# Wider conversions of the gated block's input weights, and Gram products of a block diagonal k, in a recurrence with two mixing blocks

## The chip, the cores and the metric

The kernel runs on one core of one Trainium2 chip, in one launch. The metric is the device time of that launch in microseconds (us), the median over several runs. The engines are named as the profile names them: PE is TensorE (PEld its weight loads), DVE is VectorE, ACT is ScalarE, POOL is GpSimd, SP is SyncE, which issues the transfers.

## The reference

Three stages follow each other, all in float32. The first is a recurrence with a state of 48x48 for each of 4 batches and 8 heads, over 768 steps:

```python
k_n = k / (np.linalg.norm(k, axis=-1, keepdims=True) + 1e-06)
for t in range(S):
    kt, vt, bt = (k_n[:, :, t], v[:, :, t], beta[:, :, t, None])
    y[:, :, t] = np.einsum('bhd,bhde->bhe', q[:, :, t], state)
    v_old = np.einsum('bhde,bhd->bhe', state, kt)
    state = state + bt[:, :, :, None] * np.einsum('bhd,bhe->bhde', kt, vt - v_old)
```

The second is a gated block: h = relu(x @ w_in) with w_in of 384 x 1024; half of h is u, the other half is normalized over its 512 columns, mixed over the 768 tokens by w_spatial, shifted by b_spatial and multiplied by u; the product goes through w_out. The third forms theta = x @ w_theta, mixes x cos(theta) and x sin(theta) over the tokens by two 768 x 768 matrices, adds x, and adds relu(u @ w_ch).

## The kernel before

**The recurrence in chunks.** The 768 steps are cut into 12 chunks of 64 for each batch, 48 chunks in all, counted g = 0 to 47; all 8 heads are worked on together, two on each half of the 128 partitions as four pairs (HP = 4). Eight chunks make a round (RM = 8), so there are six rounds. For a round, `norms` forms the norms of k, `gram` forms the products of k with k (and with q) within a chunk, and `invert` inverts all the round's unit triangular matrices at once on VectorE, row by row (L730 and L742). For a chunk, `chain` does what really depends on the chunk before: ru from the state (L842, L843), rt (L846), the solve with the inverse in GX (L853, L854), copies into W, the update of the state s (L869, L871), copies back into W, and the output py (L881, L882). Here "the solve" of a chunk is L853 and L854, and rt stands just ahead of it.

**Gram products.** In rounds 0 and 1 a Gram has 64 columns. From round 2 on (`FUSE = 2`) it is fused: k times k and k times q in one product of 128 columns, for 32 chunks. For each of the four pairs there are two matmuls, one on the upper left and one on the lower right quarter of the array (L670 to L672). A matmul on f32 operands is one instruction in the program and two in the trace; a transpose, and a matmul on the rounded type float32r, is one in both.

**The gated block and the third stage.** Each large product is made of three matmuls on float32r parts (high x high, high x low, low x high) in `mm_tasks` (L982). `load_w1` brings w_in, whose values arrive as float64 words: `f64_to_f32` makes float32 out of the two 32-bit halves by one instruction on ScalarE and four on VectorE (L903, L905, L907, L909), and `split` makes the two parts (a copy on ScalarE or VectorE, a subtraction at L916 on VectorE or GpSimd). The other weights go through the same conversion in the background (`park`, tiles bgr and bgm) and lie in DRAM until the third stage reads them.

**What sets the order.** Every operation is a task with a cost, a priority and the engines that may do it. A planner (`Plan.run`) goes through them at build time with these costs, picks engine and place for each, and emits the instructions in that order. On the chip each engine works its own list in order and waits on semaphores. The attention tasks have priorities of the chunk's number, the background conversions 500 and up, the large matmuls 1000 and up. On TensorE the planner also keeps an account of how busy the array is: where it expects the clock to fall, it puts in padding transposes of the identity (`filler`, L506), or prefers a large matmul. A task's `act` and `mode` tell it how busy a product keeps the array and how the array is divided for it.

**Buffers.** Rings of buffers are shared by name: in the kernel before, the raw words of w_in lie in the ring vh (six buffers) and the float32 values in vl (six buffers).

## Time and profile before

| | |
|---|---|
| median of 3 runs | 807.64 us (804.51 to 813.95) |
| the profiled execution | 808.91 us |
| its span, first to last instruction | 807.1 us |
| mean granted TensorE clock | 0.972 of full speed |
| busy share PE, DVE, ACT, POOL | 93%, 77%, 42%, 19% |
| chain that ended last, by engine | PE 60%, DVE 23%, DMA 6%, issue 4%, ACT 4% |

The profiled execution takes 1.8 us more than its span. The shares are means over two different halves, so the profile is read by stage: rt of chunk 0 starts at 38.6 us, that of chunk 12 (the second batch) at 164.9 us, that of chunk 47 (the last) at 440.2 us, and the first matmul that writes y starts at 493.0 us. A busy share of TensorE holds the latency of each matmul, so two starts are compared where a cost is wanted.

### The profile page before, as it was taken

The page shows a single profiled execution, that of the slowest core. Times are in us where ns is not written, and L with a number is a line of the kernel's source. Part 1 is how long each engine was busy: PE and PEld are TensorE (multiplying, and loading weights), DVE is VectorE, ACT ScalarE, POOL GpSimd, SP SyncE. Part 2 cuts the span into 40 slices and gives each one's busy share as a digit, 9 for nine tenths or more (in the row PEclk, how much of TensorE's full clock was granted, in tenths as well). Part 3 has the DMA queues.
Part 4 walks back from the last instruction along what each step waited for, and adds up shares of the span by engine and source line. Part 5 has one row for each costly group of instructions (what it writes and reads, how often), then busy time and mean ns, then how long its engine had stood idle before and what let it go on. Part 6 is the DMA issues. An engine that isn't in the chain of part 4 may idle for free.

```text
span 807.1 us, 21948 instructions
## 1 busy us (share of the span) xinstructions
PE 749.4 (93%) x8904; PEld 684.7 (85%) x8904; DVE 622.8 (77%) x1543; ACT 342.3 (42%) x763; POOL 155.9 (19%) x175
## 2 busy tenths in 40 slices
PE   5289889999999989999999999999999999999998
PEld 5277668778987867888878999999999999999997
DVE  5999998999997898998887564779566575556545
ACT  3636336536424444642755243355333342333321
POOL 2026622533112232211111000012111111111100
PEclk9799889999998998999999999999999999999999
DMA  7726624464575876578785710153010011002001
GB/s 219 219 65 191 177 83 140 130 171 130 185 217 171 236 230 193 156 217 245 211 240 174 222 57 14 66 175 119 20 67 27 28 42 58 26 24 75 1 1 59
DMA packets 84996, 102.42 MB, mean 127 GB/s; under 512 B 8992, under 2 KB 65568, under 8 KB 84896
## 3 DMA queue, kind: packets, MB, share of 16 engines
q1 hardware_dynamic: 84896, 101.03, 42.1%
q8 instruction: 70, 1.15, 0.6%
q14 instruction: 30, 0.25, 0.1%
HBM read 74.38 MB, written 22.41 MB: 120 GB/s over the span
## 4 chain that ended last, share of the span: by engine, by line
PE 60%; DVE 23%; DMA 6%; issue 4%; ACT 4%; SPq 2%; POOL 1%; POOLq 0%; DVEq 0%; ACTq 0%
PE m L982 29%; PE y L982 19%; DVE un L742 5%; DVE tmp L730 4%; PE mg L506 2%; PE gp L672 2%; DMA bgr<-in_w_r_dram 2%; ACT GX L474 2%; PE py L881 1%; PE ru L853 1%; DVE kq L800 1%; PE ru L842 1%; DVE GX L683 1%; DVE bgm L907 1%; PE s L869 1%
## 5 line engine op out<-in xcount | busy, mean ns | idle before, releaser
L982 PE MATMUL m<-w,vh 128*128 128x256 f32 x576 | 110.8, 292 | 0.2 <-ACT uT L474 0.2
L982 PEld LDWEIGHTS m<-w,vh 128*128 128x128 f32 x576 | 89.7, 192 | 3.5 <-issue 0.9
L982 PE MATMUL y<-wr,xTh 128*128 128x384 f32 x432 | 86.2, 337 | 0.0
L982 PE MATMUL y<-w,xTl 128*128 128x384 f32 x432 | 83.9, 336 | 0.0
L982 PE MATMUL m<-w,vl 128*128 128x256 f32 x288 | 81.9, 284 | 0.8 <-POOL vl L916 0.5
L982 PEld LDWEIGHTS y<-wr,xTh 128*128 128x128 f32 x432 | 75.3, 188 | 0.0
L982 PEld LDWEIGHTS y<-w,xTl 128*128 128x128 f32 x432 | 75.1, 188 | 0.0
L742 DVE TENSOR_TENSOR un<-un,tmp 128x30 f32<-128x30 f32 (+21 forms) x209 | 69.2, 342 | 1.1
L730 DVE TENSOR_TENSOR tmp<-un 128x30 f32<-128x30 f32 (+21 forms) x209 | 65.2, 322 | 1.2
L982 PEld LDWEIGHTS m<-w,vl 128*128 128x128 f32 x288 | 55.3, 192 | 1.2 <-POOL vl L916 0.7
L1301 DVE TENSOR_SCALAR bgr<-m 128x384 int32<-128x384 f32 x22 | 12.2, 555 | 55.1 <-PE m L982 55.1
L474 ACT ACTIVATE W<-ru 64x192 f32<-64x192 f32 x88 | 28.5, 324 | 44.7 <-PE ru L854 43.5
L982 PE MATMUL m<-xTh,wih 128*128 128x256 f32 x144 | 46.3, 322 | 0.0
L982 PE MATMUL m<-wo,gh 128*128 128x384 f32 x176 | 44.7, 334 | 0.0
L650 POOL TENSOR_TENSOR gm<-mask,ng 128x256 f32<-128x256 f32 x53 | 36.4, 690 | 41.5 <-DVE pp L693 18.5
L818 POOL TENSOR_TENSOR vk<-vk,ng 128x384 f32<-128x384 f32 x25 | 24.1, 964 | 96.8 <-DMA vk<-in_vkn_dram 63.3
L853 PEld LDWEIGHTS ru<-rt,GX 64*64 64x64 f32 x384 | 26.2, 136 | 18.1 <-DVE rt L846 13.7
L853 PE MATMUL ru<-rt,GX 64*64 64x48 f32 x384 | 32.2, 224 | 9.7 <-DVE rt L846 9.0
L506 PE MATMUL mg<-ident 128*128 128x128 f32 x231 | 38.2, 302 | 3.1 <-ACT GX L474 1.4
L982 PE MATMUL m<-xTl,wih 128*128 128x256 f32 x144 | 40.6, 282 | 0.0
L982 PE MATMUL m<-xTh,wil 128*128 128x256 f32 x144 | 40.6, 282 | 0.0
L672 PE MATMUL gp<-kg 48*64 48x128 f32 x512 | 37.5, 290 | 3.2 <-DVE pp L693 1.8
(207 smaller groups left out, 2063.0 us busy)
## 6 DMA issues: line engine op xcount, KB each, us to landing
kq<-in_kqT_dram SPq DMA_DIRECT2D x96, 128.0 KB, 3.7
vk<-in_vkn_dram SPq DMA_DIRECT2D x48, 192.0 KB, 3.7
kg<-in_kqT_dram SPq DMA_DIRECT2D x32, 256.0 KB, 3.3
gd<-gt SPq DMA_DIRECT2D x24, 256.0 KB, 2.5
graw<-gd SPq DMA_DIRECT2D x24, 256.0 KB, 3.0
k<-in_vkn_dram SPq DMA_DIRECT2D x24, 192.0 KB, 3.0
xd<-xs SPq DMA_DIRECT2D x48, 96.0 KB, 2.8
xr<-xd SPq DMA_DIRECT2D x24, 192.0 KB, 3.6
```

Source lines behind the costliest of these rows:

```text
L474: nc.scalar.activation(out=out, in_=in_, func=func, **kw)
L506: nc.tensor.transpose(MGt[:, 256:384], ident.t, ident.t)
L650: eng[e].tensor_tensor(out=gm.t, in0=mask.t.unsqueeze(1).to_broadcast([128, HP, CH]), in1=ng_b[r].t[:, j, 1].unsqueeze(2).to_broadcast([12 ...
L672: mm(out=pv()[o:o + 64, hp, :], lhsT=kh, rhs=kg.t[i:i + D, :, hp, :] if fused else kh, start=True, stop=True)
L683: nc.vector.scalar_tensor_tensor(out=GXt[1][:, u0 + hp], in0=GXt[1][:, u0 + hp], scalar=ng_b[1].t[:, j, 1, hp:hp + 1], in1=mask.t, op0=ALU ...
L730: eng[e].tensor_tensor(out=t3, in0=un.t[:, k:k + 1, 0:k].to_broadcast([128, m, k]), in1=un.t[:, t0:32:st, k:k + 1].to_broadcast([128, m, k ...
L742: eng[e].tensor_tensor(out=un.t[:, t0:32:st, 0:k], in0=un.t[:, t0:32:st, 0:k], in1=t3, op=ALU.add)
L800: A(o_dve(256), lambda e, p0=p0, i=i: nc.vector.tensor_tensor(out=kq.t[p0:p0 + 64, i], in0=gpv(ps)[p0:p0 + 64], in1=gm.t[p0:p0 + 64], op=A ...
L818: lambda e: eng[e].tensor_tensor(out=vk.t, in0=vk.t, in1=ng_b[r].t[:, j].unsqueeze(3).to_broadcast([128, 2, HP, D]), op=ALU.mult), [ng_b[r ...
L853: mm(out=pu.t[64:128, hp, :], lhsT=gx[64:128, u, :], rhs=rt.t[64:128, hp, :], start=True, stop=True)
L982: mm(out=view(), lhsT=a, rhs=c, start=(start and q == 0 and s_ == 0), stop=(stop and q == tot - 1 and s_ == 2))
L1301: P.add(o_dve(DM), lambda e: nc.vector.tensor_scalar(out=ni.t.bitcast(I32), in0=th(), scalar1=1.0 / TWO_PI, scalar2=None, op0=ALU.mult), [ ...
```

## The change

There are two edits, and a third that makes room for them. The fused Gram copies k of a chunk into a tile BD of 128 x 4 x 128, whose two diagonal blocks hold the two head halves and whose other blocks stay zero; then one matmul on the whole array does what two on quarters did. The two copies go to ScalarE or GpSimd, as the planner picks. The planner's cost for a fused Gram goes from 925 to 460 ns, its `act` from 0.35 to 0.93, its `mode` from 1 (quarters) to 0 (whole array). The input weights are converted 512 columns at a time, with the raw words in the ring uT (three buffers of 4 KB a partition) and the values in whole vl buffers. The tile sr is gone (the root is written into ng), and tmp is 240 columns wide.

```diff
+    BD = single("pa", "bd", [128, HP, 128])
+    BDh = [Buf(tile_=BD.t) for _ in range(2)]
...
-    r_sr = ring("pa", "sr", [128, RM, HP], F32, 1)
...
-    r_tmp = ring("pa", "tmp", [128, 256], F32, 2)
+    r_tmp = ring("pa", "tmp", [128, 240], F32, 2)
...
+    A([("POOL", 900.0)], lambda e: nc.gpsimd.memset(BD.t, 0.0), (), BDh, -25.0, port=False)
...
-        A([("ACT", 120.0)], lambda e: act(sr.t, ss.t, ACTF.Sqrt), [ss], [sr], p0 + 0.6, crit=r < 1)
+        A([("ACT", 120.0)], lambda e: act(ng.t[:, :, 1], ss.t, ACTF.Sqrt), [ss], [ng], p0 + 0.6, crit=r < 1)
...
             for hp in range(HP):
+                if fused:
+                    mm(out=pv()[:, hp, :], lhsT=BD.t[:, hp, :], rhs=kg.t[:, :, hp, :], start=True, stop=True)
+                    continue
                 for o, i in ((64, 0), (0, 64)):
-                    kh = kg.t[i:i + D, 0, hp, :] if fused else kg.t[i:i + D, hp, :]
-                    mm(out=pv()[o:o + 64, hp, :], lhsT=kh, rhs=kg.t[i:i + D, :, hp, :] if fused else kh, start=True, stop=True)
-
-        mt = A(o_pe(925 if r >= FUSE else 490), f, [kg], [ps], pr, crit=r < 1, act=0.35 if r >= FUSE else 0.292)
+                    kh = kg.t[i:i + D, hp, :]
+                    mm(out=pv()[o:o + 64, hp, :], lhsT=kh, rhs=kh, start=True, stop=True)
+
+        if fused:
+
+            for p0, c0, bd in ((0, 64, BDh[0]), (64, 0, BDh[1])):
+                A([("ACT", d_acts(256)), ("POOL", 480.0)], lambda e, p0=p0, c0=c0: copy(e, BD.t[p0:p0 + 64, :, c0:c0 + 64], kg.t[p0:p0 + 64, 0]),
+                  [kg], [bd], pr, part=p0)
+        mt = A(o_pe(460 if fused else 490), f, [kg] + (BDh if fused else []), [ps], pr, crit=r < 1, act=0.93 if fused else 0.292,
+               mode=0 if fused else 1)
...
-    r_cvr = Ring(pools, "pm", [128, 256, 2], I32, "vh", 6)
-    r_cvr.items = r_vh.items
-    r_cvm = Ring(pools, "pm", [128, 256], F32, "vl", 6)
+    r_cvm = Ring(pools, "pm", [128, DF], F32, "vl", 6)
...
+    r_cvr = Ring(pools, "pm", [128, DF, 2], I32, "uT", 3)
+    r_cvr.items = r_uT.items
...
-        for c0 in (DF, 0):
+        for c in (DF, 0):
             for kk in range(KX):
-                for c in (c0, c0 + 256):
-                    pr = (WP0 + 0.1 * n) if n < 6 else 0.5 + 0.3 * n
...
-                    m = f64_to_f32(r_cvr.new, r_cvm.new, w_in[kk * 128:(kk + 1) * 128, c:c + 256], 256, pr)
...
+                pr = (WP0 + 0.1 * n) if n < 3 else 0.5 + 0.6 * n
+                n += 1
+                m = f64_to_f32(r_cvr.new, r_cvm.new, w_in[kk * 128:(kk + 1) * 128, c:c + DF], DF, pr)
```

Since the planner orders everything anew, the lists of all engines change. On TensorE, early in the recurrence, the list before has two Grams in a row (16 matmuls in the program, gp from kg on 64 rows) between ru of a chunk (L842, L843) and the large matmuls of the gated block (m from the parts wih and wil of w_in):

```order
L843 MATMUL ru<-W_110,kq 64x48
L842 MATMUL ru<-W_110,kq 64x48
L843 MATMUL ru<-W_110,kq 64x48
L672 MATMUL gp<-kg 64x128 x16
L982 MATMUL m<-wih_139,xTh 128x512
L982 MATMUL m<-wil_142,xTh 128x512
```

In the changed list, a Gram there (four matmuls on the whole array, from kg and bd) stands between large matmuls, which are L992 now, and the output py (L892, L893):

```order
L992 MATMUL m<-wil_144,xTh 128x512
L992 MATMUL m<-wih_141,xTl 128x512
L673 MATMUL gp<-kg,bd 128x128 x4
L892 MATMUL py<-kq,W_110 48x64
L893 MATMUL py<-kq,W_110 48x64
```

Eight matmuls of a Gram have become four, and other work stands on either side of it. On VectorE, at the start of the inversion of round 2, the list before has the conversion of w_in (vl, 256 columns) between the inversion's steps (un and tmp, L730 and L742):

```order
L905 TENSOR_SCALAR vl<-vl 128x256
L730 TENSOR_TENSOR tmp<-un 128x30
L903 TENSOR_SCALAR vl<-vl 128x256
L742 TENSOR_TENSOR un<-un,tmp 128x30
L907 SCALAR_TENSOR_TENSOR vl<-vh,vl 128x256
L730 TENSOR_TENSOR tmp<-un 128x58
L909 SCALAR_TENSOR_TENSOR vl<-vh,vl 128x256
L742 TENSOR_TENSOR un<-un,tmp 128x2x29
```

In the changed list, just ahead of the same inversion (L719 is its transpose, the former L708), the same operations are L914, L916, L918 and L920 on 512 columns:

```order
L918 SCALAR_TENSOR_TENSOR vl<-uT,vl 128x512
L916 TENSOR_SCALAR vl<-vl 128x512
L920 SCALAR_TENSOR_TENSOR vl<-uT,vl 128x512
L918 SCALAR_TENSOR_TENSOR vl<-uT,vl 128x512
L480 CAST wih_140<-vl 128x512
L920 SCALAR_TENSOR_TENSOR vl<-uT,vl 128x512
L719 STREAM_TRANSPOSE un<-GX_112 128x1024
```

There are half as many of them, twice as wide, and two blocks are converted before the inversion starts. On GpSimd the copies of k stand among the masks gm (L652, the former L650) and the scalings of vk:

```order
L652 TENSOR_TENSOR gm<-mask,ng 128x256
L480 COPY bd<-kg 64x4x64
L652 TENSOR_TENSOR gm<-mask,ng 128x256 x2
L480 COPY bd<-kg 64x4x64
L829 TENSOR_TENSOR vk<-vk,ng 128x384
L652 TENSOR_TENSOR gm<-mask,ng 128x256 x2
```

No copy of k stood on this list before.

## Rows read from the trace of the kernel before

**Rows 1.** Busy time by stage: length, then us of PE, PEld, DVE, ACT, POOL

```profile
38.60:164.90 126.30, 113.17 (x1958) 94.48 (x1956) 118.55 (x353) 59.12 (x140) 55.15 (x64) 0.93 0.46 129
164.90:440.20 275.30, 259.22 (x4377) 219.15 (x4378) 248.43 (x637) 132.31 (x308) 60.22 (x66) 0.97 0.69 201
440.20:493.00 52.80, 52.80 (x412) 50.23 (x412) 32.54 (x75) 19.95 (x38) 2.21 (x4) 1.00 0.36 111
493.00:807.10 314.10, 309.82 (x1872) 307.67 (x1871) 194.15 (x360) 110.53 (x226) 33.69 (x29) 1.00 0.16 51
```

**Rows 2.** The large matmuls (L982) alone, by stage: PE, PEld, clock, DMA

```profile
164.90:440.20 275.30, 142.99 (x814) 111.16 (x815) 0.97 0.69 201
440.20:493.00 52.80, 51.76 (x380) 49.18 (x380) 1.00 0.36 111
```

**Rows 3.** Chain that ended last, from 440 us: start, us, what

```profile
444.49 48.49 PE m L982 x354
492.98 1.05 PE y L982 x6
```

**Rows 4.** Timeline, ru of one chunk: start, us, instruction

```profile
231.44 0.22 PE L842 MATMUL ru<-W,kq 48*64 48x48 f32 x1
231.45 0.22 PE L843 MATMUL ru<-W,kq 48*64 48x48 f32 x1
...
231.50 0.22 PE L842 MATMUL ru<-W,kq 48*64 48x48 f32 x1
231.51 0.22 PE L843 MATMUL ru<-W,kq 48*64 48x48 f32 x1
```

**Rows 5.** Timeline, one fused Gram and the matmul behind it

```profile
117.45 1.09 PE L672 MATMUL gp<-kg 48*64 48x128 f32 x16
118.47 0.39 PE L982 MATMUL m<-xTh,wih 128*128 128x256 f32 x1
```

**Rows 6.** Padding transposes (L506) in two stretches: PE, PEld, clock, DMA

```profile
38.70:42.10 3.40, 3.40 (x18) 3.40 (x17) 0.50 0.00 0
42.20:46.90 4.70, 4.70 (x44) 4.52 (x42) 1.00 0.01 3
```

**Rows 7.** Groups of instructions by shape, VectorE: xcount, busy us, mean ns

```profile
L907 DVE SCALAR_TENSOR_TENSOR bgm<-bgr,bgm 128x384 int32<-128x384 int32 x34 | 22.0, 648 | 0.3
...
L903 DVE TENSOR_SCALAR bgm<-bgm 128x384 f32<-128x384 f32 x34 | 14.7, 433 | 6.8 <-ACT bgm L474 6.7
...
L916 DVE TENSOR_TENSOR vl<-hv,vh 128x512 fp32r<-128x512 f32 x14 | 9.4, 688 | 1.0 <-ACT vh L474 0.9
...
L907 DVE SCALAR_TENSOR_TENSOR vl<-vh,vl 128x256 int32<-128x256 int32 x12 | 5.4, 450 | 0.0
...
L916 DVE TENSOR_TENSOR wil<-vl,wih 128x256 fp32r<-128x256 f32 x9 | 5.2, 575 | 0.0
...
L903 DVE TENSOR_SCALAR vl<-vl 128x256 f32<-128x256 f32 x12 | 4.1, 353 | 0.0
...
L905 DVE TENSOR_SCALAR vl<-vl 128x256 int32<-128x256 int32 x12 | 3.8, 316 | 0.1
```

**Rows 8.** Subtractions for the tile gl: ns min/median/max, first and last start

```profile
L916 DVE TENSOR_TENSOR gl<-graw,gh x15: 679/1585/1691, 455.9 to 753.3; 128x512 fp32r<-128x512 f32 x15
L916 POOL TENSOR_TENSOR gl<-graw,gh x9: 1287/1290/1293, 560.9 to 753.2; 128x512 fp32r<-128x512 f32 x9
```

**Rows 9.** Padding transposes (L506) by stage: PE, PEld, clock, DMA

```profile
38.60:164.90 126.30, 35.21 (x220) 26.69 (x219) 0.93 0.46 129
164.90:440.20 275.30, 2.88 (x11) 1.30 (x11) 0.97 0.69 201
```

**Rows 10.** Waits from 100 to 440 us, PE's and DVE's longest

```profile
PE ru L853 <- DVE rt L846: 7.4, 10, 1.4
...
DVE rt L846 <- PE ru L843: 7.9, 9, 2.3
```

**Rows 11.** The tile kg: what its readers' engine waited for

```profile
  DMA kg<-in_kqT_dram: 0.2, 1
```

More of the change, by code (lines that the diff above doesn't have):

```diff
@@ L608, in norms @@
         p0 = (r - 2) * RM + NPR if r > 1 else -20.0 if r == 0 else -10.0
-        ss, sr = r_ss.new(), r_sr.new()
+        ss = r_ss.new()
         ng = ng_b[r] = r_ng.new()
@@ L626, in f2 @@
             n, ga = ng.t[:, :, 0], ng.t[:, :, 1]
-            nc.vector.reciprocal(out=n, in_=sr.t)
+            nc.vector.reciprocal(out=n, in_=ga)
             nc.vector.tensor_tensor(out=n, in0=n, in1=ss.t, op=ALU.mult)
-            nc.vector.tensor_tensor(out=n, in0=n, in1=sr.t, op=ALU.add)
+            nc.vector.tensor_tensor(out=n, in0=n, in1=ga, op=ALU.add)
             nc.vector.tensor_scalar(out=n, in0=n, scalar1=0.5, scalar2=1e-6, op0=ALU.mult, op1=ALU.add)
@@ L1019, in m_V @@
               for kk in range(KX)]
-        wr = [x for kk in range(KX) for c in (2, 3) for x in wiq[kk, c]]
+        wr = [x for kk in range(KX) for x in wiq[kk, 1]]
         mm_tasks(ps, lambda: ps.t, gr, DF, [hi, lo] + wr, pr)
@@ L1073, in m_U @@
                   for kk in range(KX)]
-            wr = [x for kk in range(KX) for x in wiq[kk, f // 2]]
+            wr = [x for kk in range(KX) for x in wiq[kk, 0]]
             mm_tasks(ps, lambda ff=ff: v3()[:, ff, :], gr, TG, [hi, lo] + wr, pr, per=UPER)
```

11 lines of the change are left out of this document (5 added, 6 removed).

## The prediction

> **What bounds the kernel now.** I read the busy time by stage first. The program has two halves. Until the 48th chunk of the recurrent part is solved (440.2 us) no engine is saturated alone: between 164.9 and 440.2 us, the last 35 chunks, VectorE is busy 248.43 of 275.3 us and TensorE 259.22 [rows 1]. From there to the end TensorE alone decides: 52.8 of 52.8 us and 309.8 of 314.1 us, with VectorE at about 62% [rows 1]. The chain of waits confirms it: one piece of 48.49 us, 354 matmuls of the gated block without a break, then the second mixing block's y [rows 3]. The waits in the first half show what the two engines do there: TensorE waits for VectorE's rt (7.4 us), VectorE for TensorE's ru (7.9 us) [rows 10]. Neither queue runs ahead of the other; the recurrence passes between them, and each has other work standing in front of it.
>
> So the time is the moment of the last solve plus the TensorE work still left then. A large matmul (L982) before that moment fills a hole; one after it costs its full 51.76 / 380 = 0.136 us [rows 2].
>
> **Gram products.** Before, each fused Gram issues 16 instructions on 64x64 quarters, two at a time: in the rows of ru, which have the same form with 48 columns, two instructions on opposite quarters start 0.01 us apart and the next pair 0.06 us later [rows 4]. A Gram of 16 takes 118.47 - 117.45 = 1.02 us until the next matmul starts [rows 5], so eight pairs at some 0.11 us and the edges. After, 8 full-array instructions of 128 columns. The trace has such a thing, the padding transposes on the identity, 128x128 in f32: 44 in 4.70 us at full clock, 0.107 us each, and 18 in 3.40 us at half [rows 6]. Eight of those are 0.86 us. The two quarters already ran side by side, and a full-array instruction takes as long as a pair. The edges depend on neighbours and I count none: the new product stands among quarter-sized matmuls as often as the old one stood among large ones. Bounds: 0.46 us saved per Gram if the diff's figure (460 instead of 925) were true, 32 x 0.46 = 14.9 us; nothing saved, or some tenths lost, if weights of 128 columns are not hidden. I take zero, the transposes being the nearest row and carrying 128-column weights themselves.
>
> The Trainium skill, TensorE: Matmul & The Clock Gate, section Back-to-back issue gap, gives N/2.4 + 2.5 ns between matmuls, 56 ns for 128 columns; by it the new Gram would be 0.45 us and the sum some 14 us lower. The 0.107 us of the transposes speaks against it for f32.
>
> Against that stands new work: 64 half copies of k into the block diagonal tile, 33 on ScalarE and 31 on GpSimd in the program's order. ScalarE is busy 132.31 of 275.3 us [rows 1], which hides its share. If a ScalarE copy waits for k or for the earlier Gram, the copies of W stand behind it, and the recurrence with them; k lands early enough now (the Gram waited 0.2 us for it in all) [rows 11], so I add nothing. GpSimd is not free of cost: when it subtracts for gl, VectorE's own subtraction for gl has a median of 1585 ns where its shortest is 679 [rows 8]. Bounds for 31 copies: nothing, if they fall beside VectorE work that reads PSUM, and 31 x 0.91 = 28 us at the gl rate. I take 1 us, near the lower end: a copy is half as wide on half the partitions, and the order spreads the copies over 32 chunks.
>
> The Trainium skill, GPSIMD Engine Reference, section Specifications, says that GpSimd shares its SBUF interfaces with VectorE and collides with instructions that have two SBUF inputs; most of the inversion is of that kind. By that rule alone the upper bound is the nearer one; the gl rows agree with its direction, and no row has the price of such a copy.
>
> **Input weights.** Twelve conversions of 256 columns become six of 512. On VectorE: 12 x (353 + 316 + 2 x 450) ns = 18.8 us, taking L909 like L907, plus 9 subtractions of 575 ns = 5.2 us, in all 24.0 us [rows 7]. The wider forms by the step from 256 to 384 columns, 80 ns for L903 and 198 ns for L907 [rows 7], taken twice: 6 x (513 + 476 + 2 x 846) = 16.1 us, plus 4 subtractions at 688 ns = 2.8 us, 18.9 us. Saved: 5.1 us, all before chunk 12, where VectorE is busy 118.55 of 126.3 us [rows 1]. The order puts 77 more transposes on TensorE (308 for 231), nearly all before chunk 12, 77 x 0.107 = 8.2 us. They are meant for idle time, and 220 are there now [rows 9]; but TensorE cannot skip them when its wait ends early. Bounds for this stretch: -5.1 to +8.2 us. I take -1: VectorE is the busier engine there. ACT's square root now writes into ng; same count, same size, nothing.
>
> **What moves.** The order is made anew by the planner's costs, and this is larger than either edit. Counted in it, between the first solve of chunk 12 and that of chunk 47, VectorE has 580 instructions where it had 635, and TensorE 744 large matmuls where it had 825 (in the whole program 3096 both times). Twenty Grams lie in this stretch both times. At 248.43 / 637 = 0.390 us [rows 1] the 55 instructions are 21.4 us; the 81 matmuls at 0.136 are 11.0 us. So the last solve comes earlier by between 11 us (TensorE's load decides) and 21 us (VectorE's). I take 16, the middle, because the waits go both ways in nearly equal parts [rows 10]. The bill comes after: 852 large matmuls stand before the last solve where 930 stood, 78 x 0.136 = 10.6 us more at the end, all uncovered. VectorE's work there grows as well, four more background conversions; it has some 20 us idle between 440 and 493 [rows 1], which hides them.
>
> Sum, against the profiled execution's 808.9 us (span 807.1; the median of the runs is 807.6): -1 - 16 + 1 + 0 + 10.6 = -5.4, so 803.5 us; near the median's level I say 803.
>
> **Rivals.** VectorE's load decides. Then the full 5.1 and 21.4 us are gained and 10.6 given back: 808.9 - 15.9 = 793 us. For it: VectorE at 94% and 90% in the two stretches. Against: TensorE has the greater share from 164.9 us on.
>
> The Grams do halve: 32 x 0.46 = 14.9 us less on TensorE, 803.5 - 14.9 = 789 us if all of it reaches the chain. For it: nothing but the diff's own cost. Against: rows 4 to 6.
>
> Slower: the order is packed for Grams of 0.46 us that take 0.87. TensorE works its queue in order, so each Gram pushes the recurrence's matmul behind it by 0.41 us, 32 x 0.41 = 13.1 us, and VectorE, short of work in front of its own waits, cannot make it up. The chain then gains 17 - 13.1 = 3.9 us only, and the 10.6 us at the end remain: 808.9 - 3.9 + 1 + 10.6 = 816.6 us. It decides once the last solve comes less than about 11 us earlier (before 429 us is the break-even). For it: TensorE's 259.22 of 275.3 us leave few holes. Against: part of that share is waiting inside the pipeline, and a Gram is no predecessor of the same chunk's solve.
>
> **How the numbers follow.** The forecast 0.47; VectorE decides 0.20; Grams halve 0.13; slower 0.20. One per cent, 8 us, is about what a measurement of this kernel tells from no change. The forecast's own range is 797 to 812 us, within 1%. The first two rivals are faster by more than 1%, the last slower by about 1%: 0.33, 0.47, 0.20. The range to hold 8 in 10 reaches down to the VectorE case and up to the slower one: 792 to 816 us; the halved Grams and a POOL collision at its upper bound are left out.
>
> **What would show it.** In the profile after: the first large matmul run without a break starting near 425 us (429 breaks even, 415 is VectorE's case); the stretch from there to the first y near 63 us instead of 52.8; Gram rows of 8 at 0.85 to 1.0 us for the Gram, and not 0.46; 308 transposes; conversion rows of 512 columns near 510, 480 and 850 ns. A longer rt row, or inversion rows that grew, would put the loss on GpSimd's copies. The forecast is wrong if the last solve comes at 430 us or later, or if TensorE has holes after it.

## The result, and the profile after

The changed kernel takes 814.12 us (median; 808.04 to 817.83), the kernel before 806.5 us beside it: 1.0086 of before, 95% interval 1.0060 to 1.0112. It is slower, by a little under 1%; the forecast was 803 us and no change. The profiled execution takes 817.35 us, its span is 815.5 us. Of two kernels below, those with the planner's 935 and 905, two of four and seven of ten runs were disturbed by a lower clock, so that their ratios rest on two and three runs and their profiles are not used.

Busy time by stage of the changed kernel, cut at the same events as [rows 1]: rt of chunks 0, 12 and 47, then the first y. The columns are length, then us of PE, PEld, DVE, ACT, POOL, then the clock, the DMA share and GB/s.

```profile
39.00:170.60 131.60, 119.13 (x1918) 102.78 (x1917) 123.86 (x328) 66.07 (x150) 56.94 (x69) 0.95 0.41 119
170.60:432.40 261.80, 249.65 (x4167) 213.50 (x4168) 228.30 (x581) 137.16 (x318) 72.58 (x91) 0.97 0.70 204
432.40:502.10 69.70, 66.06 (x483) 62.29 (x484) 48.42 (x107) 26.79 (x53) 11.32 (x9) 0.95 0.38 122
502.10:815.50 313.40, 309.61 (x1873) 307.47 (x1872) 194.44 (x360) 110.67 (x227) 33.43 (x29) 1.00 0.16 52
```

Against [rows 1] the four stages are 5.3 longer, 13.5 shorter, 16.9 longer and 0.7 us shorter, together 8.0; the start is 0.4 us later. That is the whole 8.4 us between the spans. The second stage is the gain that was forecast; the third takes more than all of it back.

This is one execution. Six versions below keep the changed kernel's order in nearly every place (e1, e2, e6, e8, e13, e18); their profiled executions have chunk 12 at 169.0 to 171.7 us, the last solve at 426.1 to 430.7 us and a third stage of 66.7 to 70.6 us. The late chunk 12, the gain behind it and the loss after it are in all of them; a difference of 2 or 3 us between two single profiles is not read as an effect here.

**After the last solve.** The chain that ended last, before and in the unbroken run of large matmuls (start, us, what):

```profile
435.07 0.19 PE py L892
435.70 0.60 ACT xs L474
436.30 0.48 ACT xTh L474
436.78 0.23 SPq L900
437.06 4.72 DMA xd<-xs
441.87 4.77 DMA cvm<-wdo
446.67 0.48 ACT xTh L474
447.15 0.44 ACT bgm L474
447.59 0.82 ACT wo L474 x2
448.42 0.52 ACT vh L474
448.94 0.41 ACT wo L474
449.35 0.49 ACT uT L474
449.88 52.33 PE m L992 x366
502.22 1.05 PE y L992 x6
```

Before, that run began 4.3 us after the last solve [rows 1, 3]; now it begins 17.5 us after it, and behind a row of ScalarE instructions, each waiting its turn. TensorE's timeline there (start, us, instruction, and in brackets the idle time before it and what ended it):

```profile
445.97 0.28 PE L992 MATMUL m<-w,vl 128*128 128x256 f32 x1
449.88 0.80 PE L992 MATMUL m<-w,vh 128*128 128x256 f32 x2 [3.64 <-ACT uT L474]
```

Before, TensorE was busy in all 52.80 us of this stage [rows 1]; now it stands idle for 3.64 us in one piece, until an eviction on ScalarE (uT) frees the PSUM buffer that it needs. ScalarE's longest waits in the 12 us around it:

```profile
ACT bgm L474 <- DMA bgr<-in_w_ch_dram: 2.4, 1, 2.4
ACT sd L474 <- DVE td L1044: 1.3, 1, 1.3
ACT hv L474 <- DVE nb L1052: 1.3, 1, 1.3
```

The first is a background conversion that waits for its load, the other two are the layer norm (td, sd, nb, hv) of the third batch's last value blocks, which the next large matmuls (w times vh) need. And the clock there, by windows:

```profile
445.00:449.00 4.00, 1.25 (x11) 1.04 (x9) 3.86 (x13) 3.08 (x7) 1.84 (x1) 1.00 1.00 367
449.00:456.00 7.00, 6.12 (x28) 6.00 (x29) 6.64 (x6) 3.85 (x8) 6.72 (x5) 0.51 0.67 201
456.00:462.00 6.00, 6.00 (x53) 6.00 (x53) 5.19 (x10) 0.00 (x0) 0.00 (x0) 1.00 0.55 181
```

TensorE is nearly idle for 4 us, and in the next 7 us its clock is granted at half (1.2 GHz of 2.4). Behind that, at full clock, 53 matmuls take 6.00 us, 0.113 us each; at that rate the 28 would have taken 3.2 us and not 6.12, so about 2.9 us go there. With the 3.64 us of the wait that is about the part of the 16.9 us that the moved matmuls (10.6 us) do not explain. The DMA engines are busy all through the idle 4 us (share 1.00), and the chain above passes through two transfers of 4.72 and 4.77 us; whether fewer loads there would shorten the wait was not tried.

**Ahead of chunk 12.** VectorE is the busier engine here, 123.86 of 131.60 us, and it has 5.3 us more work than before although the conversions became cheaper. The converted columns first (mean ns of one, to be held against [rows 7]), then the inversion, before and after:

```profile
L918 DVE SCALAR_TENSOR_TENSOR vl<-uT,vl 128x512 int32<-128x512 int32 x6 | 6.3, 1046 | 0.0
L920 DVE SCALAR_TENSOR_TENSOR vl<-uT,vl 128x512 int32<-128x512 int32 x6 | 4.1, 679 | 0.0
L927 DVE TENSOR_TENSOR wil<-vl,wih 128x512 fp32r<-128x512 f32 x4 | 3.9, 984 | 0.0
L916 DVE TENSOR_SCALAR vl<-vl 128x512 int32<-128x512 int32 x6 | 3.3, 550 | 0.0
L914 DVE TENSOR_SCALAR vl<-vl 128x512 f32<-128x512 f32 x6 | 2.9, 497 | 0.0
```

```profile
L742 DVE TENSOR_TENSOR un<-un,tmp 128x84 f32<-128x84 f32 (+23 forms) x58 | 20.5, 362 | 0.3
L730 DVE TENSOR_TENSOR tmp<-un 128x84 f32<-128x84 f32 (+22 forms) x57 | 18.4, 332 | 0.3
```

```profile
L753 DVE TENSOR_TENSOR un<-un,tmp 128x84 f32<-128x84 f32 (+20 forms) x64 | 24.0, 382 | 0.5
L741 DVE TENSOR_TENSOR tmp<-un 128x84 f32<-128x84 f32 (+20 forms) x64 | 21.7, 346 | 0.5
```

The conversions now cost 20.5 us in all, where they cost 23.7 (5.4, 5.2, 4.1, 3.8 and 5.2 us for L907, L909, L903, L905 and L916). The inversion has 128 instructions in this stage where it had 115, and 45.7 us where it had 38.9. The 13 more are of round 2, whose inversion starts at 143.6 us before and 143.9 us after; they stand ahead of chunk 12 because chunk 12 is late, and do not make it late.

What does, as far as the trace shows, is the inversion of round 1 (chunks 8 to 15). Its last transpose on VectorE and the first matmul of the solve of chunk 8, which needs the inverse, before and after:

```profile
118.18 1.95 DVE L750 STREAM_TRANSPOSE GX<-un 128x1024 f32<-128x1024 f32 x1
134.19 0.25 PE L853 MATMUL ru<-rt,GX 64*64 64x48 f32 x1
```

```profile
141.53 1.95 DVE L761 STREAM_TRANSPOSE GX<-un 128x1024 f32<-128x1024 f32 x1
149.01 0.25 PE L864 MATMUL ru<-rt,GX 64*64 64x48 f32 x1
```

This inversion starts at 65.8 us before and 66.6 us after, and ends 23.4 us later than before. Chunk 8 itself is not late (its rt starts at 132.3 us before, 131.7 us after), but its solve follows 1.9 us behind rt before and 17.3 us behind it now; on TensorE it starts right behind the last block products of the inverse (mg L779, at 148.72 us). By chunk 12, 5.7 us of this are left. In all versions below that keep this order the inversion of round 1 ends at 141.8 to 145.7 us.

**Gram products.** One fused Gram after, and the matmul behind it:

```profile
163.71 1.16 PE L673 MATMUL gp<-kg,bd 128*128 128x128 f32 x8
164.86 0.25 PE L864 MATMUL ru<-rt,GX 64*64 64x48 f32 x1
```

From the start of a Gram to the next matmul it is 0.99 us in the median of 32 (0.91 to 1.16), against 1.02 us in [rows 5]. Half the instructions, and the same time.

### The profile page after: what moved, and what is told of

It is laid out like the page before. It is cut to its first block, busy times and chain, and to the rows that moved or that the text cites. A ratio compares the mean times of both kernels' runs of the same rounds, so it can differ in the third digit from the quotient of the medians.

```text
span 815.5 us, 21644 instructions
## 1 busy us (share of the span) xinstructions
PE 761.4 (93%) x8725; PEld 702.2 (86%) x8725; DVE 624.9 (77%) x1495; ACT 360.5 (44%) x795; POOL 181.0 (22%) x214
## 4 chain that ended last, share of the span: by engine, by line
PE 66%; DVE 20%; DMA 7%; ACT 4%; issue 2%; SPq 1%; POOL 0%; POOLq 0%; DVEq 0%; ACTq 0%
PE m L992 32%; PE y L992 19%; DVE un L753 4%; DVE tmp L741 4%; PE mg L506 2%; PE ru L864 2%; DMA bgr<-in_w_i_dram 2%; PE gp L673 2%; PE py L892 2%; PE s L880 1%; DMA xd<-xs 1%; DMA vk<-in_vkn_dram 1%; PE ru L853 1%; ACT GX L474 1%; PE mg L785 1%
## 5 line engine op out<-in xcount | busy, mean ns | idle before, releaser
L992 PE MATMUL m<-w,vh 128*128 128x256 f32 x576 | 115.0, 299 | 3.6 <-ACT uT L474 3.6
L992 PEld LDWEIGHTS m<-w,vh 128*128 128x128 f32 x576 | 92.1, 197 | 6.5 <-ACT uT L474 3.8
L992 PE MATMUL y<-wr,xTh 128*128 128x384 f32 x432 | 86.2, 337 | 0.0
L992 PE MATMUL y<-w,xTl 128*128 128x384 f32 x432 | 84.0, 337 | 0.0
L992 PE MATMUL m<-w,vl 128*128 128x256 f32 x288 | 83.2, 289 | 0.0
L992 PEld LDWEIGHTS y<-wr,xTh 128*128 128x128 f32 x432 | 75.3, 188 | 0.0
L992 PEld LDWEIGHTS y<-w,xTl 128*128 128x128 f32 x432 | 75.1, 188 | 0.0
L753 DVE TENSOR_TENSOR un<-un,tmp 128x30 f32<-128x30 f32 (+21 forms) x209 | 72.5, 357 | 1.2
L741 DVE TENSOR_TENSOR tmp<-un 128x30 f32<-128x30 f32 (+21 forms) x209 | 69.3, 342 | 1.4
L992 PEld LDWEIGHTS m<-w,vl 128*128 128x128 f32 x288 | 56.5, 196 | 0.1
L506 PE MATMUL mg<-ident 128*128 128x128 f32 x308 | 48.1, 307 | 5.6 <-ACT GX L474 3.2
L474 ACT ACTIVATE W<-ru 64x192 f32<-64x192 f32 x82 | 26.7, 326 | 51.5 <-PE ru L865 47.6
L506 PEld LDWEIGHTS mg<-ident 128*128 128x128 f32 x308 | 39.2, 157 | 8.1 <-ACT GX L474 3.7
L992 PE MATMUL m<-xTh,wih 128*128 128x256 f32 x144 | 45.1, 313 | 0.0
L992 PE MATMUL m<-wo,gh 128*128 128x384 f32 x176 | 44.7, 334 | 0.0
L829 POOL TENSOR_TENSOR vk<-vk,ng 128x384 f32<-128x384 f32 x30 | 28.7, 958 | 64.1 <-DMA vk<-in_vkn_dram 49.7
L652 POOL TENSOR_TENSOR gm<-mask,ng 128x256 f32<-128x256 f32 x53 | 36.0, 684 | 29.7 <-DVE kq L811 13.2
L992 PE MATMUL m<-xTl,wih 128*128 128x256 f32 x144 | 40.9, 284 | 0.0
L992 PE MATMUL m<-xTh,wil 128*128 128x256 f32 x144 | 40.9, 284 | 0.0
```

The lines of the kernel that those rows point to most:

```text
L474: nc.scalar.activation(out=out, in_=in_, func=func, **kw)
L506: nc.tensor.transpose(MGt[:, 256:384], ident.t, ident.t)
L652: eng[e].tensor_tensor(out=gm.t, in0=mask.t.unsqueeze(1).to_broadcast([128, HP, CH]), in1=ng_b[r].t[:, j, 1].unsqueeze(2).to_broadcast([12 ...
L741: eng[e].tensor_tensor(out=t3, in0=un.t[:, k:k + 1, 0:k].to_broadcast([128, m, k]), in1=un.t[:, t0:32:st, k:k + 1].to_broadcast([128, m, k ...
L753: eng[e].tensor_tensor(out=un.t[:, t0:32:st, 0:k], in0=un.t[:, t0:32:st, 0:k], in1=t3, op=ALU.add)
L829: lambda e: eng[e].tensor_tensor(out=vk.t, in0=vk.t, in1=ng_b[r].t[:, j].unsqueeze(3).to_broadcast([128, 2, HP, D]), op=ALU.mult), [ng_b[r ...
```

## The experiments

The table puts the order of each kernel beside its time. "Ahead" is the number of large matmuls ahead of the last solve, of 3096; "pads" the padding transposes; both are counted in the program. The three moments are read from the timeline of one profiled execution (rt of chunks 12 and 47, first y). The first y of the kernel before starts at 492.8 us; the cut at 493.0 us in [rows 1] follows the chain's row of it. In e5 the first y comes before the gated block has ended, so its moment says nothing of the end.

| kernel | ahead | pads | chunk 12 | last solve | first y | of before, 95% interval |
|---|---|---|---|---|---|---|
| before | 930 | 231 | 164.9 | 440.2 | 492.8 | 1 |
| after | 852 | 308 | 170.6 | 432.4 | 502.1 | 1.0086, 1.0060 to 1.0112 |
| e1 quarters | 852 | 308 | 171.3 | 429.4 | 500.0 | 1.0131, 1.0078 to 1.0184 |
| e2 no copies | 852 | 308 | 169.0 | 430.4 | 497.9 | 1.0079, 1.0042 to 1.0115 |
| e13 old work | 852 | 308 | 171.1 | 426.1 | 494.2 | 1.0053, 1.0018 to 1.0088 |
| e8 fewer pads | 852 | 232 | 171.7 | 427.6 | 494.7 | 1.0060, 1.0029 to 1.0091 |
| e18 less background | 852 | 308 | 170.7 | 430.7 | 497.4 | 1.0064, 1.0026 to 1.0101 |
| e6 early eviction | 852 | 308 | 170.7 | 430.5 | 501.1 | 1.0103, 1.0040 to 1.0167 |
| e16 early layer norm | 852 | 308 | 169.4 | 434.4 | 507.2 | 1.0169, 1.0113 to 1.0226 |
| e17 the same, fewer pads | 852 | 232 | 174.3 | 429.9 | 502.1 | 1.0149, 1.0084 to 1.0215 |
| e3 Gram edit alone | 954 | 296 | 174.4 | 453.9 | 503.0 | 1.0125, 1.0069 to 1.0181 |
| e4 conversions alone | 930 | 306 | 172.5 | 444.4 | 496.5 | 1.0099, 1.0066 to 1.0132 |
| e9 root in ng alone | 954 | 245 | 166.4 | 442.6 | 491.7 | 0.9993, 0.9946 to 1.0040 |
| e5 after, Gram cost 900 | 789 | 279 | 174.4 | 441.5 | 467.1 | 1.0302, 1.0248 to 1.0356 |
| e12 after, Gram cost 480 | 879 | 319 | 177.2 | 450.6 | 509.2 | 1.0260, 1.0172 to 1.0348 |
| e7 before, belief of after | 930 | 297 | 165.9 | 435.4 | 487.5 | 0.9955, 0.9926 to 0.9985 |
| e15 e7 with Gram cost 480 | 930 | 243 | 168.7 | 443.4 | 495.3 | 1.0087, 1.0050 to 1.0124 |
| e14 e7, fewer pads | 930 | 229 | 169.8 | 442.1 | 494.6 | 1.0035, 1.0009 to 1.0061 |
| e10 before, Gram cost 935 | 846 | 271 | | | | 1.0129, 0.9996 to 1.0261 |
| e11 before, Gram cost 905 | 930 | 217 | | | | 1.0036, 0.9957 to 1.0115 |

### Is it the new work? The old work in the new order

Three kernels keep the changed kernel's order, instruction by instruction, and put the old work back step by step: first the quarters, then no copies (the tile bd is not needed for quarters), then the narrow conversions.

```diff
-                    mm(out=pv()[:, hp, :], lhsT=BD.t[:, hp, :], rhs=kg.t[:, :, hp, :], start=True, stop=True)
+                    mm(out=pv()[o:o + 64, hp, :], lhsT=kh, rhs=kg.t[i:i + D, :, hp, :], start=True, stop=True)
```

> The changed kernel with every list in the same order, but each fused Gram issued as before, as 16 instructions on quarters; the copies of k are still made (nothing reads them). Theory (a full-array f32 instruction of 128 columns takes as long as a pair on two quarters, 0.107 against 0.11 us): the same time as the changed kernel, 814 us, within 3 us; a Gram takes 0.85 to 1.05 us in both. Rival (the full-array form is really half as long, 0.46 us): 5 to 14 us longer, 819 to 828 us.

> As the run with quarters, and the 64 copies of k are not issued; every other instruction keeps its place. Theory (the copies lie beside other work): within 2 us of the run with quarters. Rival (31 copies on GpSimd hold up VectorE, 33 on ScalarE hold up the copies of W): 5 us or more shorter, 809 us or less, with shorter inversion rows.

```diff
+        hs = ((0, 256), (256, 512)) if n == DF else ((0, n),)
...
-        P.add([("ACT", d_acts(n))], lambda e: act(m.t, hi().bitcast(F32), ACTF.Abs), [raw], [m], pr)
+        P.add([("ACT", d_acts(n))], each(lambda a, b: act(m.t[:, a:b], hi(a, b).bitcast(F32), ACTF.Abs)), [raw], [m], pr)
```

> The changed kernel's own order, task by task, with the work of the kernel before issued at each place: the Gram products on quarters, no copies into bd, and every 512-column load, conversion and split of the gated block's input weights issued as two of 256 columns. What is left of the change is the order, the root in ng and the ring that the converted columns lie in. Theory C (the order that the planner drew is the loss): 811 to 818 us, 0.6 to 1.4% above before, with last solve at 428 to 434 and a stretch of 66 to 71 us after it. Theory A (the changed work is the loss, the order is not): within 0.3% of before.

1.0131, 1.0079 and 1.0053. Giving up the full array gains nothing, so a full-array product takes as long as a pair of quarters; at 817.42 us the time lies between what the two sides expected, and its interval overlaps that of the changed kernel. The copies may be worth about half a per cent; the two intervals overlap, and 3.3 us less is again between the two sides. With all of the old work back the kernel is still 0.5% slower than before, with the changed kernel's marks: the inversion of round 1 ends late (143.9 us), chunk 12 is late, the last solve early, 68.1 us from there to y, and a wait in the same place, though with no half clock behind it (longest waits of TensorE in e13 between the two):

```profile
PE m L1011 <- ACT uT L474: 3.0, 1, 3.0
PE m L1011 <- POOL vl L945: 0.9, 1, 0.9
```

So at least a part of the loss, some 0.5 of 0.86%, is the order, with the root in ng (which costs nothing, see e9) and the buffer ring of the converted words, which e13 keeps. Its expected range, 811 to 818 us, was met at its edge (811.16 us); the last solve, at 426.1 us, came earlier than the 428 to 434 expected.

### Is it one of the edits? Each alone

> The Gram edit alone (block diagonal k, its copies, its planner costs, the root written into ng); the input weights converted 256 columns at a time as before. The planner orders it anew: 954 large matmuls stand before the solve of chunk 47 (930 before the change, 852 in the changed kernel). Theory A (the late start of the early chunks comes from the wide conversions, the hole at the end from this one order): rt of chunk 1 near 64 us instead of 72.8, no hole after the last solve, 800 to 808 us. Theory B (the planner's too small cost for the Gram is the loss): 812 us or more, with the last solve hardly earlier than 440 us.

> The conversion edit alone (512 columns, raw words in uT, the root written into ng, tmp of 240); Grams on quarters with the planner's old costs. 930 large matmuls before the solve of chunk 47, as before the change. Theory A (wide conversions delay the early chunks): rt of chunk 1 near 73 us, and the whole 808 to 816 us. Theory B (the Gram's cost is the loss): the conversion's saving is kept, 800 to 807 us.

```diff
-        A([("ACT", 120.0)], lambda e: act(sr.t, ss.t, ACTF.Sqrt), [ss], [sr], p0 + 0.6, crit=r < 1)
+        A([("ACT", 120.0)], lambda e: act(ng.t[:, :, 1], ss.t, ACTF.Sqrt), [ss], [ng], p0 + 0.6, crit=r < 1)
```

> The kernel before, with only the part that the Gram edit and the conversion edit both carried: the square root is written into the second half of the norms' own tile ng and the ring sr is gone, and the scratch of the inversion holds 240 columns. Gram products and conversions are those of before. By the order 954 large matmuls stand ahead of the last solve (930 before) and 245 padding transposes run (231 before). Theory S (the shared part is what made either edit alone 1% slower: the root has to wait for a buffer that is handed on later): 812 to 816 us, with chunks 12 to 47 about 10 us longer. Theory C (each change makes the planner draw another order, and what the order places where decides, not the work): last solve later by 24 x 0.136 = 3.3 us and the stretch after it shorter by the same, 804 to 809 us unless the drawn order has a hole of its own.

Each edit alone costs as much as both together, 1.0125 and 1.0099, and by different ways: the Gram edit has its last solve 13.7 us later and no hole behind it, the conversions 4.2 us later. What the two share, the root in ng, costs nothing (0.9993). By its time e3 came out as its theory B, e4 as its theory A, and these two exclude each other; and rt of chunk 1 starts at 66.3 and 62.5 us (63.6 before, 72.8 in the changed kernel), so the wide conversions by themselves do not delay the early chunks, as e4's theory had it. In e3 and e4 the inversion of round 1 ends late again, at 141.0 and 137.5 us; in e9 it ends at 124.6. Losses that neither add up nor stay in one place are hardly the price of an operation.

### Is it the planner's wrong belief? Telling it otherwise

The slower rival said that the order is packed for Grams of 460 ns that take 870. Two kernels turn that belief alone: the changed kernel with a cost of 900, and the kernel before with the changed kernel's three figures.

```diff
-        mt = A(o_pe(460 if fused else 490), f, [kg] + (BDh if fused else []), [ps], pr, crit=r < 1, act=0.93 if fused else 0.292,
+        mt = A(o_pe(900 if fused else 490), f, [kg] + (BDh if fused else []), [ps], pr, crit=r < 1, act=0.93 if fused else 0.292,
```

> The changed kernel with the planner's cost of a fused Gram at 900 ns, near what the trace shows (0.91 to 1.09 us), in place of 460; everything is ordered anew, with 789 large matmuls before the last solve and 279 transposes. Theory B (the wrong cost is the loss): 798 to 808 us. Theory A (the order's other features are the loss, the cost is of little weight): 810 us or more; with 63 large matmuls fewer before the last solve, that must come 8.6 us earlier than 432.4 us only to break even with the changed kernel.

```diff
-        mt = A(o_pe(925 if r >= FUSE else 490), f, [kg], [ps], pr, crit=r < 1, act=0.35 if r >= FUSE else 0.292)
+        mt = A(o_pe(460 if fused else 490), f, [kg], [ps], pr, crit=r < 1, act=0.93 if fused else 0.292, mode=0 if fused else 1)
```

> The kernel before, with the planner's three figures for a fused Gram alone taken from the change (460 instead of 925 ns, act 0.93, mode 0); the Grams stay on quarters, without copies, and the weights are converted 256 columns at a time. Theory B (an order packed for half-length Grams loses time): slower than the kernel before by 4 to 10 us, 811 to 817 us. Theory A (the figure matters little): within 4 us of the kernel before.

The truth made the changed kernel much slower (1.0302), the false figures made the old one faster (0.9955, the whole interval below 1). Both go against the rival. But each is also one new order, and the next section has the old kernel with the same false figures, but for 20 ns, at 1.0087; so the rival is not borne out, and not excluded as a part. The version with the false figures is the one that beats both kernels; its stages up to the first y:

```profile
38.10:165.90 127.80, 114.24 (x1965) 97.16 (x1963) 117.06 (x347) 60.10 (x141) 54.30 (x63) 0.96 0.46 130
165.90:435.40 269.50, 254.88 (x4441) 217.25 (x4442) 246.90 (x635) 135.25 (x308) 73.35 (x72) 1.00 0.69 202
435.40:487.50 52.10, 52.10 (x408) 49.53 (x407) 33.40 (x76) 19.43 (x37) 2.55 (x4) 1.00 0.38 121
```

The second stage is 5.8 us shorter than that of [rows 1]. In this execution the clock is at full speed throughout it, where it was 0.97, but the version does not need that to be faster: its ten executions have mean clocks of 0.977 to 0.994, and at 0.978 it took 801.97 and 802.24 us, at 0.994, in the profiled one, 803.37.

### How much is a draw worth? One number altered, no instruction

If the order is the loss, another order of the same instructions must give another time. Four kernels alter the planner's cost of a Gram by 20 ns or less; the order changes, and the number of padding transposes with it.

```diff
-        mt = A(o_pe(925 if r >= FUSE else 490), f, [kg], [ps], pr, crit=r < 1, act=0.35 if r >= FUSE else 0.292)
+        mt = A(o_pe(935 if r >= FUSE else 490), f, [kg], [ps], pr, crit=r < 1, act=0.35 if r >= FUSE else 0.292)
```

> The kernel before with one number of the planner's alone: the length that it assumes for a paired Gram product is 935 ns instead of 925. No instruction is added, removed or altered; their order is. 846 large matmuls stand ahead of the last solve (930 before, 852 in the changed kernel) and 271 padding transposes run (231 before, 308 in the changed kernel). Theory C (the redrawn order is the loss): the time moves by several us with no edit at all, and in the way of the changed kernel: last solve at 429 to 434 (84 x 0.136 = 11.4 us earlier at most, 40 x 0.107 = 4.3 us of padding against it), stretch from it to the first output matmul at least 52.6 + 11.4 = 64, 70 if it also runs dry there; 806 to 814 us. Theory A (the edits' own work, waits and buffers are the loss): what is moved costs after the last solve what it saves ahead of it, 804 to 808 us.

> The kernel before with the planner's length for a paired Gram product at 905 ns instead of 925, no instruction altered. 930 large matmuls ahead of the last solve as before, 217 padding transposes (231 before). Theory C: the count ahead of the last solve is the same and fewer transposes pad, so within 1% of before, 800 to 809 us, but not the same time. Theory A: the time of before, 805 to 807 us.

> The changed kernel with the planner's length for a Gram product at 480 ns instead of 460, no instruction altered. 879 large matmuls ahead of the last solve (852 in the changed kernel, 930 before), 319 padding transposes (308). Theory C: another draw, 27 large matmuls back ahead of the last solve, so last solve 3.7 us later, stretch after it 3.7 us shorter, and the hole there smaller or gone; anywhere in 805 to 820 us, and not the 814 of the changed kernel. Theory A: the edits' work is unchanged, so 813 to 815 us.

> The kernel before with the planner's three Gram figures at 480 ns, share 0.93, mode 0 (the version at 460 took 0.9955 of before); quarters, no copies, no instruction altered. 930 large matmuls ahead of the last solve and 243 padding transposes (930 and 297 at 460). Theory C in full (the gain at 460 was the luck of one draw): another time, anywhere within 799 to 815 us. Theory B' (a planner that takes Grams for short packs better): 798 to 804 us, as at 460.

The two that redraw the kernel before are not told from it with certainty (their intervals include 1). The other two are: 480 for 460 takes the changed kernel from 1.0086 to 1.0260, and the faster version from 0.9955 to 1.0087, both with intervals far apart. How little was foreseen: e12 took 828.61 us, above the expected 805 to 820, and its last solve came 18.2 us later than the changed kernel's, not 3.7. e15 has 930 large matmuls ahead like e7, so that count does not explain it. It has 54 padding transposes fewer, and the section on the padding shows that 68 fewer alone cost 0.8%, so they may be a part of its 1.3%. Either way the gain of e7 was a lucky draw and no merit of the false figures, which e15 shares, and the loss of the changed kernel, 0.9%, is no larger than what an altered number makes without any edit.

One mark goes with the time. In every kernel whose inversion of round 1 ends at 137.5 us or later (after, e1 to e6, e8, e12, e13, e16 to e18) chunk 12 starts at 169.0 us or later, and the kernel is 0.5 to 3.0% slower than before. In before, e7 and e9 it ends at 120.1 to 124.6 us, and chunk 12 starts at 164.9 to 166.4. In e14 and e15 it ends at 129.1 and 121.2 us and chunk 12 starts at 169.8 and 168.7, with a clock of 0.90 and 0.84 in that stage. No run moved the inversion alone.

### Is it the padding?

```diff
-        for _ in range(n):
+        for _ in range(n if n == BURST0 else min(n, 8)):
             nc.tensor.transpose(MGt[:, 256:384], ident.t, ident.t)
```

> The changed kernel with every run of padding transposes cut to 8 (the first run of 60 stays), 232 in all instead of 308; every other instruction keeps its place. Theory (76 transposes at 0.107 us stand ahead of the early chunks' matmuls, and cost up to 8 us there): rt of chunk 12 starts 4 to 8 us earlier than 170.6 us, and the whole takes 3 to 8 us less, 806 to 811 us. Rival (they lie in time in which TensorE would wait anyway, or they hold the clock up): chunk 12 as late as now or later, 813 to 818 us.

> The kernel before with the planner's three Gram figures of the changed kernel (460 ns, share 0.93, mode 0), quarters and no copies, which took 0.9955 of before, and each run of padding transposes but the opening one cut to 8: 229 transposes instead of 297. If padding takes TensorE time that work is waiting for, 68 x 0.107 = 7 us less at most, 796 to 802 us; if it fills time that is idle anyway, 802 us as without the cut; if the clock falls for want of it, 803 to 808 us.

In the changed kernel 76 transposes fewer leave chunk 12 where it was (171.7 us), so they were not its delay; the ratio of 1.0060 is not told from 1.0086. In the faster version 68 fewer make it slower, 1.0035 for 0.9955 (809.96 us, a little above the 803 to 808 of the third case). The mean clock is 0.964 to 0.976 in its twelve executions, where it was 0.977 to 0.994 in the ten of e7. Its first two stages:

```profile
38.20:169.80 131.60, 112.83 (x1913) 95.28 (x1911) 116.80 (x346) 59.51 (x141) 53.31 (x63) 0.90 0.45 127
169.80:442.10 272.30, 257.65 (x4422) 219.69 (x4423) 248.17 (x635) 134.15 (x308) 71.72 (x72) 0.97 0.69 200
```

They are 3.8 and 2.8 us longer than those of e7, with a clock of 0.90 for 0.96 and 0.97 for 1.00. The padding earned its time there. That it does so by way of the clock is likely and not shown: within the executions of e7 the time does not follow the clock.

### What makes the hole after the last solve?

Four attempts on the changed kernel's order: one eviction of uT issued seven places earlier on ScalarE; the last value blocks with their layer norm issued ahead of an up-projection (36 matmuls) instead of behind it; the same with fewer pads; and four background conversions beside them left out.

> The changed kernel with one ScalarE instruction moved ahead by seven places in its list: the relu that frees the PSUM buffer for which TensorE waits 3.6 us at 446 us; nothing else moves. Theory (the hole after the last solve and the half clock that follows it cost 3.6 and 2.6 us): 6 us shorter than the changed kernel, 808 us, with no hole at 446 us and no half clock at 449 to 456 us. Rival (the next wait takes its place, or the third stage's start waits for something else): 812 to 814 us.

```diff
+    def early(self, out):
+        V = [t for t in at if lab.get(t) in (("V", 2, 4), ("V", 2, 5))]
+        U = [t for t in at if lab.get(t) and lab[t][:3] == ("U", 2, 1)]
...
+        for t, k in zip(V, vs):
+            pos[t] = k
+        for t, k in zip(U, us):
+            pos[t] = k
```

> The changed kernel with one exchange in its order and no instruction altered: the 36 matmuls of the third batch's last two value blocks, their evictions and the layer norm behind them are issued ahead of the 36 matmuls of the preceding up-projection instead of behind them, so that the layer norm can start 36 x 0.136 = 4.9 us earlier against the work that needs it. Theory H (of the 9 us after the last solve that the forecast had not, 6.4 are TensorE running dry behind that layer norm for 3.6 us and the half clock that follows): no wait over 1 us between the last solve and the first output matmul, no half clock there, stretch 69.7 -> 63 to 65 us, 807 to 810 us. Rival (as when one eviction alone was moved: the next wait takes its place, or the earlier layer norm holds up the recurrence on VectorE by as much): stretch shorter but last solve later, or a wait of 3 us left; 812 to 816 us.

> As e16_ln_early, and each run of padding transposes but the opening one cut to 8 (232 instead of 308), which alone took the changed kernel from 1.0086 to 1.006 of before. If the two losses are apart and add: another 2 to 4 us off, 804 to 808 us, no slower than before. If the padding keeps the clock up that the early layer norm needs, or fills idle time: as e16_ln_early or slower.

```diff
+            if t is not None and t.tag and t.tag[0] == "conv" and t.tag[2] in (513.5, 516.0, 517.0):
+                t.fn = t.tag[3]
```

> The changed kernel with the conversion of four 384-column pieces of background weights left out (parts of w_i and w_ch): the four that stand, on ScalarE and VectorE, among the last value blocks of the third batch and their layer norm. In place of each one's ScalarE instruction and four VectorE instructions stands one VectorE memset; loads, stores and every other instruction and its place are those of the changed kernel. TensorE's list is unaltered. Theory H2 (TensorE runs dry after the last solve because these conversions, the first of which waits 2.4 us for its load in ScalarE's queue, stand ahead of the layer norm's steps and the evictions): the wait of 3.6 us falls to 1.5 us or less and the half clock behind it goes, stretch 69.7 -> 63 to 66 us, 806 to 811 us. Rival (the layer norm itself is too long for the work that stands beside it): a wait of 2.5 us or more stays, 811 to 815 us.

The longest waits of TensorE after the last solve in e6, e16 and e18, in this order:

```profile
PE m L1008 <- POOL vl L943: 3.5, 1, 3.5
```

```profile
PE m L1039 <- ACT uT L521: 5.4, 2, 4.6
```

```profile
PE m L1013 <- ACT uT L492: 2.0, 1, 2.0
```

With the eviction moved, the wait has the same length and another releaser: the subtraction that ends the layer norm. Moving the whole layer norm ahead made things worse than even its rival said (820.13 us, a wait of 4.6 us, a stage of 72.8 us), and with fewer pads as well (e17, 818.88 us): the value blocks need buffers that are not free yet (ScalarE's evictions into hv wait 2.5 us for VectorE's vl), ScalarE works its list in order, and behind the moved steps stand evictions and background conversions that wait for their loads (ScalarE's waits in e16, from 425 us):

```profile
ACT bgm L521 <- DMA bgr<-in_w_ch_dram: 4.0, 3, 1.8
...
ACT xTh L521 <- DMA xr<-xd: 3.1, 1, 3.1
```

Without the four conversions the wait falls from 3.64 to 1.97 us, and the stage is 66.7 us instead of 69.7. A half clock still follows, for 3.5 us where it lasted 6.8:

```profile
446.30:449.80 3.50, 3.50 (x15) 3.33 (x16) 3.44 (x5) 1.54 (x3) 3.50 (x4) 0.51 0.67 207
```

But e2 and e8, which keep the four conversions, have waits of 2.7 and 2.4 us and stages of 67.5 and 67.1 us. So it is not shown that the background conversions are a part of the hole, and neither side of that expectation was met in full. The time, 1.0064, is not told from 1.0086, and no version of this order without the hole was found.

## Why the prediction was wrong

The sum was -1, -16, +1, 0 and +10.6 us; the profile shows +5.3 up to chunk 12, -13.5 from there to the last solve, and +16.9 behind it. Two terms failed, both to the same side. The stated range of 792 to 816 us holds the 814.12, but only because it was drawn out to the slower rival, whose story the runs do not bear out.

- **Gram products, right.** "The two quarters already ran side by side, and a full-array instruction takes as long as a pair." Measured 0.99 for 1.02 us, and no gain from undoing it. By the formula of the Trainium skill (TensorE: Matmul & The Clock Gate, Back-to-back issue gap), which the page gives for an isolated matmul without the time for its weights, 0.45 us would be the estimate. The Gram's own rows now speak against it for f32, as the transposes did.
- **Copies, right within what can be told.** I took 1 us for them on GpSimd; leaving all 64 out is worth half a per cent, with overlapping intervals, and the upper bound of 28 us is excluded. The sign that I named for them, inversion rows that grew, did come: in the first two stages the instructions on un take 155.34 us where they took 148.79. But without a copy they still take 153.97 us (e2) and 155.17 us (e13), so it is a sign of the order and not of the copies.
- **Up to chunk 12, wrong by 6.3 us.** "I take -1: VectorE is the busier engine there." The step that failed is to price this stage by VectorE's sum of work. The conversions saved 3.2 us and not 5.1, because the slowest of the wide forms took 1046 and 984 ns where I had 846 and 688. But the sum is not what decides: the solve of chunk 8 waits for the inversion of round 1, and that ends at 143.5 us where it ended at 120.1. I had looked at no single result that the recurrence waits for. Of the 55 instructions that VectorE loses between chunk 12 and the last solve, which I booked as gain, 14 are inversion instructions that now fall ahead of the late chunk 12, and behind the last solve it has 32 more than before; I did not ask where they went.
- **Chunk 12 to the last solve, nearly right.** 13.5 us for 16, between the bounds, nearer to TensorE's 11. In the six other profiles of this order it is 13.9 to 20.2 us.
- **After the last solve, wrong by 6.3 us.** The 78 matmuls at 0.136 us were right as far as they go. "VectorE's work there grows as well, four more background conversions; it has some 20 us idle ..., which hides them." By the stage rows VectorE has 107 instructions there for 75 and 48.42 us for 32.54; among them is a layer norm that the next large matmuls wait for, and four background conversions stand beside it on ScalarE and VectorE. TensorE waits 3.64 us there and loses about 2.9 us more at half clock. Idle time in the sum over a stage covers nothing in the 4 us where a chain passes through. What in those lists makes the wait stays open. I had named the sign of it ("if TensorE has holes after it") and not looked for it in the order.
- **The slower rival** gave 816.6 us and asked for a last solve at 429 us or later; both came (817.35 us profiled, 432.4 us). Yet e5 and e7 do not bear out its mechanism. A right number is no evidence for the story that gave it.
- **The chances.** I treated the order as a consequence of the edits. The runs show that it is drawn anew by any edit, and that a draw alone, with the padding that comes with it, is worth from 0.9955 to 1.0087 of before; 0.20 for slower was too little for a change whose own work comes to nothing.

What stays open: how the remaining 0.3% divide between copies, wide conversions and chance; what lets the inversion of round 1 end so late in the new order; and what an order with only that put right would take. That the solve of chunk 8 waits for it is read from the traces and was not tried.

## What to carry to other kernels

Where a greedy planner sets the order, an edit is two changes, its work and a new draw; alter one cost by a few per cent with no instruction changed, and see how far the time moves, before crediting or blaming an edit for 1%. Book the moved work at both ends: what leaves one stretch stands in another, and what lands behind the last point of the critical recurrence is priced by its dependent chain there, not by its count. Ahead of that point, too, ask which result of the busy engine the recurrence waits for, and when the new order delivers it. When a wait's releaser is moved away and the wait stays with another releaser, look at what all of them queue behind.

## What the runs showed of the hardware that was not expected

Instructions of one shape differ by what runs beside them. Of the twelve 128x512 shifts and merges on VectorE (L918 and L920) eight took 676 to 680 ns and four, all on L918, 1028 to 1486 ns; in e4 all twelve took 673 to 684. Each of the four began while an instruction on GpSimd was running, and ended 0.55 us after it; none of the eight began so. One of the four, with its neighbour:

```profile
63.90 1.31 POOL L829 TENSOR_TENSOR vk<-vk,ng 128x384 f32<-128x384 f32 x1 [0.86 <-DMA vk<-in_vkn_dram]
64.45 1.31 DVE L918 SCALAR_TENSOR_TENSOR vl<-uT,vl 128x512 int32<-128x512 int32 x1
```

The 418 steps of the inversion show the same: beyond the shortest of their form they take 16.9 us in all before and 24.4 us after, and 14.3 and 21.5 us of that fall on those that began while GpSimd worked.

Padding transposes are not only filler. From 38.66 us on nothing but these transposes ran on TensorE, and its clock rose from half to full at 42.1 us [rows 6]; 68 fewer of them in the faster version left it a mean clock of 0.964 to 0.976 for 0.977 to 0.994 and cost 0.8%, while 76 fewer in the changed kernel cost nothing that can be told. And a wait of TensorE is not always followed by a half clock: behind e13's 3.0 and 0.9 us the clock stays at full, behind e18's 1.97 us it is at half for 3.5 us.
